# Pooled attention and two MLPs in 3xFP32r on one core: storage of the seven weight forms, weight rings, row copies and batch 1's pooled sums

## The chip, the cores and the metric

The kernel runs on one core of a Trainium2 chip. The metric is the device time of one execution in microseconds (us). Three runs of the kernel before took 1726.25, 1720.11 and 1726.49 us, a median of 1726.25 us.

## The reference

```python
# attention: 8 batches, 8 heads, 576 rows, head 64; keys and values are averaged over 8 rows
k_p = k.reshape(B, H, 72, 8, 64).mean(axis=3)
v_p = v.reshape(B, H, 72, 8, 64).mean(axis=3)
scores = q @ k_p.T / 8;  attn = softmax(scores);  x = attn @ v_p      # x: 4608 tokens x 512
# first MLP (512 -> 2048 -> 512)
h = x @ w_in
y = where(h >= 1, h, where(h <= -1, 0, (h + 1) ** 2 / 4)) @ w_out
# second MLP (512 -> 1536 -> 512)
out = (sigmoid(y @ w_gate) * (y @ w_val)) @ w_out2
```

## The kernel before, in words

Tokens are worked on in nine blocks of 512. An FP32 product is made of three FP32r matmuls: each operand is split into a high and a low part, and `three` (lines 603 to 607) multiplies high by high, high by low, low by high. So nearly every operand costs one copy on ScalarE (the high part) and one subtraction on VectorE (the low part) before TensorE can use it.

**No order is written out.** The program registers operations in a `Plan` with an engine, a cost, a key (the time at which it is due) and the buffers that it reads and writes. `Plan.issue` then simulates the engines with these costs and puts the operations out in the order that it finds: on each engine, among those that could start, the one with the lowest key. The real engines follow that order strictly, each in its own queue. A buffer of a ring (`Buf` with a tag and a number of copies) is taken in the order in which the program created the buffers, unless `fifo=False`: line 98 makes a first user of a ring wait, in the plan, for the first user of the buffer created before it.

The stages, with the stretch of the profiled execution that each takes:

- **To about 165 us, batch 0 and block 0.** `pooled` (line 315) sums keys and values over groups of 8 rows. For batches 0 and 1 (`PE_SUMS = 1`) one transfer loads all 8 rows and TensorE adds them up against an identity matrix (line 349 for keys, line 370 for values). For batches from 2 on, SP loads the first 4 rows (line 328), a transfer on POOL's queue adds the other 4 rows to them (line 329, `accum_op=ALU.add`), and VectorE sums the remaining 4 (line 335). Meanwhile the weights of the first MLP arrive 8 bytes a value and are converted (`weight`, line 550); a copy of each goes back to memory on POOL's queue (line 594), and the buffer f of w_in's conversion, one of 3, comes free when that copy has landed. Block 0's second GEMM runs in plain FP32 (line 735).
- **165 to 710 us, blocks 1 to 6 of the first MLP**, with the attention of the later blocks between their steps. At the end of a block the four PSUM banks `acc` go through two buffers of the ring `raw` to memory (`out_rows`, line 617; `raw` has 2 copies of 4 KB per partition and also takes raw weights and the operands of `prepare1`). The next block's first accumulation waits for the copies at lines 622 and 623.
- **710 to 860 us, block 0 of the second MLP.** `prepare` (line 818) also makes the seven sums of quarters ("forms") of each pair of gate or value column blocks that Strassen's scheme (Winograd's form) needs, splits them, and stores them with one transfer (line 849). Per partition the DRAM tensor holds all seven high parts and then all seven low parts, so a later load of one form (`load_seven`, line 853) takes two runs of 1 KB from each partition.
- **From 860 us, pairs.** Four more rounds use Strassen's scheme on two blocks at a time: 7 products in place of 8. Round 0 ("in") runs blocks 7 and 8 through the first MLP, rounds 1 to 4 ("gv") run pairs of blocks through the second. In a round, `load_one` or `load_seven` fetch one form into the ring `ws` (9 buffers of 256 KB); then `out_pair` (line 964) does the second GEMM with the out weights' forms, loaded by line 982 into the ring `wo` (5 buffers). Each `ws` or `wo` buffer serves 6 matmuls. The splits of the activations are lines 793 and 794, the sums of halves line 970; `A` (line 967) sets how far ahead of the product the split is due: 12 for round 0, 30 for the others.
- **In round 1** (about 1020 to 1145 us) `prepare_out` (line 935) also builds the seven forms of the out weights: 6 times it reloads 512 KB into a `raw` buffer (line 942, due 12 ahead of its sums), sums (line 946), splits into `wo` buffers and stores (line 956, POOL's queue). In every round `input_sums` (line 1124) makes the next round's sums of inputs, twice, each time holding one `raw` buffer and the buffer `bt` (loads at line 1131, stores at line 1138); the next round reads them back at line 1217 and splits them at lines 788 and 789.

Of the kernel before, what the change touches and what calls it, by code (L numbers as in the profile page):

```python
# [18 lines left out]
P = 128  # L19
POOL = 8  # L20
# [22 lines left out]
AHEAD_SPLIT = 12.0  # L43
# [30 lines left out]
class Plan:  # L74
# [7 lines left out]
    def op(self, eng, cost, key, fn, r=(), w=(), after=(), behind=(), nbytes=0, share=1.0, dmas=1):  # L82
        o = Op()
        o.ways = [(eng, cost, fn)] if isinstance(eng, str) else list(zip(eng, cost, fn))
        o.key, o.bytes, o.share, o.dmas = key, nbytes, share, dmas
        o.takes, data, order = [], set(after), set(behind)
        for b in r:
            data |= set(b.writers)
            b.readers.append(o)
        for b in w:  # L90
            if b in r:
                data |= set(x for x in b.readers if x is not o)
            elif b.readers:
                data |= set(b.readers)
                b.readers, b.writers = [], []
            if b.ring and not b.users:
                o.takes.append(b)
                if b.fifo and b.ring in self.last:
                    order.add(self.last[b.ring])
                self.last[b.ring] = o  # L100
            elif b.ring:
                order.add(b.users[0])
            b.writers.append(o)
        for b in set(r) | set(w):
            b.users.append(o)
# [100 lines left out]
def pooled_attention_two_mlps(  # L206
# [75 lines left out]
    AC = {n: ac for n in ("kp", "q", "qT", "mx", "sm", "aq", "aT")}  # L282
# [20 lines left out]
    def due1(s):  # L303
        return T0 + S1 * s
# [10 lines left out]
    def pooled(b, p, T):  # L315
        h0 = 2 * p

        def kv():
            if b == 0:
                return Buf(x_p, "x", 2 * KD, [C, 2, POOL, D], fifo=False)  # L320
            return Buf(kv_p, "kv", 2, [C, 2, POOL if b <= PE_SUMS else POOL // 2, D])

        def load(src, o, key):
            rows = src[b, h0:h0 + 2].rearrange("h (c r) d -> c h r d", r=POOL)
            if b <= PE_SUMS:
                op(SP, 0.475, key, lambda: nc.sync.dma_start(out=o.t, in_=rows), w=[o], nbytes=C * 4096)
# [12 lines left out]
        ks, vs = kv(), kv()  # L339
        kt, vp = kts[b % 2, p], vps[b % 2, p]  # L340
# [3 lines left out]
        if b <= PE_SUMS:  # L344

            def add_keys():
                for r in range(POOL):
                    for h in range(2):
                        nc.tensor.matmul(out=pt.t[D * h:D * h + D, 0:C], lhsT=ks.t[:, h, r], rhs=ident.t[:C, :C],
                                         start=r == 0, stop=r == POOL - 1)  # L350
            op(PE, 1.1, T + 1, add_keys, r=[ks, ident], w=[pt], share=0.3)
# [13 lines left out]
        if b <= PE_SUMS:  # L365
            pv = bank(where)

            def add_values():
                for r in range(POOL):
                    nc.tensor.matmul(out=pv.t[:C, 0:P].rearrange("c (h d) -> c h d", h=2), lhsT=ident.t[:C, :C],  # L370
                                     rhs=vs.t[:, :, r], start=r == 0, stop=r == POOL - 1)
            op(PE, 1.8, T + BEHIND_V, add_values, r=[vs, ident], w=[pv], share=0.6)
# [244 lines left out]
    def out_rows(key, dst, accs, d=()):  # L617
        for i in range(2):
            st = Buf(raw_p, "raw", 2, [P, 2, TB])
# [54 lines left out]
    for j in range(NB1):  # L674
# [66 lines left out]
        out_rows(due1(s + 2) - 4, y_d[j].t, accs, [y_d[j]])  # L741
# [71 lines left out]
    def buf_seven():  # L813
        tag, bufs = (("wa", 2), ("wa", 2), ("wb", 1))[turn[0] % 3]
        turn[0] += 1
        return late(tag, bufs, [P, 2, NMAT, HK], F32R)

    def prepare(n, i, key):
# [4 lines left out]
        def lo(k, k1=None):  # L823
            return sl.t[:, 1, k:k1].bitcast(F32) if k1 else sl.t[:, 1, k].bitcast(F32)
# [21 lines left out]
        split2(key - 3, lambda: sl.t[:, 0, 0:3], lambda: sl.t[:, 1, 0:3], 1.0, sl)  # L846
        split_to(key - 1, lambda: sm.t, lambda: sl.t[:, 0, 3:], lambda: sl.t[:, 1, 3:], 1.3, sm, sl)
        d = seven[2 * i + n]
        op2(PL, 1.0, key + 1, lambda: nc.gpsimd.dma_start(out=d.t, in_=sl.t.rearrange("p s k f -> p (s k f)").bitcast(F32)),
# [3 lines left out]
    def load_seven(n, i, mat, key):  # L853
        w, d = late("ws", 9, [P, 2, HK], F32R), seven[2 * i + n]
        op2(SP, 0.475, key, lambda: nc.sync.dma_start(
            out=w.t.bitcast(F32), in_=d.t.rearrange("p (s k f) -> p s k f", s=2, k=NMAT)[:, :, mat]), r=[d], w=[w], nbytes=P * 2 * HK * 4)
# [37 lines left out]
    for i in range(MP):  # L894
# [4 lines left out]
        for n in range(2):  # L899
            sl, a21 = slots[n]  # L900
            for f in range(2):
                last = []
                for c in range(KD):
                    def mm(c=c, sl=sl, a21=a21, o=banks[n, f], f=f):
                        k = slice(c % 2 * P, c % 2 * P + P)
                        a = [a21.t[:, s, k] if (f, c // 2) == (1, 0) else
                             sl.t[:, s, {(0, 0): 0, (0, 1): 1, (1, 1): 2}[f, c // 2], k] for s in range(2)]
# [27 lines left out]
    def prepare_out(i, key):  # L935
# [5 lines left out]
        for n, d in enumerate((d1, d2)):  # L941
            op2(SP, 0.475, key - 12, lambda n=n, d=d: nc.sync.dma_start(
# [21 lines left out]
    def out_pair(pr, hs, K0, KP):  # L964
        kind, j1, j2 = pairs[pr]
        MP = len(hs)
        A = AHEAD_SPLIT if kind == "in" else 30
# [383 lines left out]
```

## Time and profile before

| what | value |
|---|---|
| runs, us | 1726.25, 1720.11, 1726.49 |
| the profiled execution's own time, us | 1720.69 |
| its span, first to last instruction, us | 1718.8 |
| mean granted TensorE clock | 0.996 |
| matmuls | 8720 |
| DMA traffic | 400.30 MB, mean 233 GB/s, 348713 packets |

The profile is of one execution. A line of it names an engine (PE is TensorE, PEld its weight loads, DVE is VectorE, ACT is ScalarE, POOL is GpSimd, SP the queue that issues most transfers), a line of the kernel, the tile written and the tiles read, and times. A wait is put down to what ended it: `PE acc L605 <- ACT raw L622` is a matmul of line 605 that waited for a copy of line 622. A `q` behind an engine's name means its queue: a waiting or issuing instruction.

### The profile page before, as it was taken

How to read it: one execution, taken by the hardware profiler on the slowest of the kernel's cores; microseconds unless marked ns; L12 is line 12 of the kernel's file. 1: busy time of each engine (PE TensorE's matmuls, PEld its weight loads, DVE VectorE, ACT ScalarE, POOL GpSimd, SP SyncE). 2: the span in 40 equal slices, each digit the busy share in tenths (PEclk: the TensorE clock that was granted, in tenths of full speed). 3: DMA queues.
4: the chain of work that ended last, by engine and by line, in shares of the span. 5: the costliest groups of instructions: out<-in, count | busy, mean ns of one | idle time of the engine just before them, and what ended most of it. 6: DMA issues, size and time to landing. Idle time of an engine off the chain costs nothing.

```text
span 1718.8 us, 26738 instructions
## 1 busy us (share of the span) xinstructions
PE 1686.4 (98%) x8720; PEld 1334.7 (78%) x8720; DVE 1173.1 (68%) x2197; ACT 976.5 (57%) x2173; POOL 223.2 (13%) x346
## 2 busy tenths in 40 slices
PE   7999999999999999999999999999999999999998
PEld 6665777777777777778887787778888888888886
DVE  5896777788887878856767946565447545744476
ACT  5764656676676767654466745464435444544344
POOL 0112221323434122200000002100000000000000
PEclk8999999999999999999999999999999999999999
DMA  8975655777887766648988869997889788867774
GB/s 218 301 216 147 153 133 143 204 213 211 237 240 198 221 194 227 223 153 315 342 278 243 272 206 356 343 367 205 241 248 295 220 239 271 273 202 203 208 219 136
DMA packets 348713, 400.30 MB, mean 233 GB/s; under 512 B 133408, under 2 KB 254240, under 8 KB 347040
## 3 DMA queue, kind: packets, MB, share of 16 engines
q1 hardware_dynamic: 312320, 287.15, 56.3%
q0 software_dynamic: 36256, 111.45, 19.6%
q8 instruction: 70, 1.15, 0.3%
q14 instruction: 67, 0.55, 0.1%
HBM read 276.30 MB, written 112.72 MB: 226 GB/s over the span
## 4 chain that ended last, share of the span: by engine, by line
PE 77%; DMA 11%; DVE 5%; issue 3%; ACT 2%; SPq 2%; POOL 1%; DVEq 0%; POOLq 0%; ACTq 0%
PE h L605 10%; PE h L607 10%; PE h L606 10%; PE acc L605 9%; PE acc L607 9%; PE acc L606 9%; PE a L605 5%; PE a L606 5%; PE a L607 5%; PE acc L735 3%; DMA raw<-in_moe_w_out_dram 2%; DMA q<-in_q_dram 2%; PE a L502 1%; DMA seven<-f 1%; DMA raw<-in_moe_w_gate_dram 1%
## 5 line engine op out<-in xcount | busy, mean ns | idle before, releaser
L794 DVE TENSOR_TENSOR g<-win,g 128x512 fp32r<-128x512 f32 x168 | 114.6, 688 | 120.4 <-ACT g L793 119.4
L605 PE MATMUL h<-x,win 128*128 128x512 f32 x448 | 184.4, 412 | 1.2 <-DVE t L718 1.2
L607 PE MATMUL h<-x,win 128*128 128x512 f32 x448 | 175.0, 391 | 1.2 <-DVE win L537 1.2
L606 PE MATMUL h<-x,win 128*128 128x512 f32 x448 | 175.1, 391 | 0.0
L793 ACT CAST g<-win 128x512 fp32r<-128x512 f32 x168 | 104.3, 623 | 112.9 <-PE acc L607 94.5
L605 PE MATMUL acc<-g,wo 128*128 128x512 f32 x400 | 156.5, 391 | 3.9 <-ACT g L793 2.0
L606 PE MATMUL acc<-g,wo 128*128 128x512 f32 x400 | 155.9, 390 | 0.4 <-DVE g L794 0.2
L607 PE MATMUL acc<-g,wo 128*128 128x512 f32 x400 | 155.7, 389 | 0.0
L605 PE MATMUL acc<-g,wj 128*128 128x512 f32 x384 | 153.9, 401 | 1.6 <-ACT raw L622 1.6
L606 PE MATMUL acc<-g,wj 128*128 128x512 f32 x384 | 150.2, 391 | 0.0
L607 PE MATMUL acc<-g,wj 128*128 128x512 f32 x384 | 149.8, 390 | 0.0
L605 PE MATMUL h<-x,ws 128*128 128x512 f32 x336 | 131.2, 390 | 1.5 <-ACT h L1295 0.8
L606 PE MATMUL h<-x,ws 128*128 128x512 f32 x336 | 131.0, 390 | 0.6 <-DVE x L789 0.6
L607 PE MATMUL h<-x,ws 128*128 128x512 f32 x336 | 130.8, 389 | 0.0
L713 ACT ACTIVATE t<-h,half 128x512 f32<-128x512 f32 x112 | 77.0, 687 | 77.9 <-PE h L607 75.3
L605 PEld LDWEIGHTS h<-x,win 128*128 128x128 f32 x448 | 84.1, 188 | 31.0 <-issue 7.9
L607 PEld LDWEIGHTS h<-x,win 128*128 128x128 f32 x448 | 84.1, 188 | 20.0 <-DVE win L537 1.6
L606 PEld LDWEIGHTS h<-x,win 128*128 128x128 f32 x448 | 84.2, 188 | 18.0 <-issue 2.4
L605 PEld LDWEIGHTS acc<-g,wo 128*128 128x128 f32 x400 | 75.1, 188 | 22.9 <-ACT g L793 2.8
L605 PEld LDWEIGHTS acc<-g,wj 128*128 128x128 f32 x384 | 72.0, 188 | 22.5 <-issue 3.0
L606 PEld LDWEIGHTS acc<-g,wo 128*128 128x128 f32 x400 | 75.1, 188 | 16.4 <-DVE g L794 1.1
L607 PEld LDWEIGHTS acc<-g,wo 128*128 128x128 f32 x400 | 75.1, 188 | 15.7
(296 smaller groups left out, 4040.8 us busy)
## 6 DMA issues: line engine op xcount, KB each, us to landing
ws<-seven SPq DMA_DIRECT2D x392, 256.0 KB
wo<-seven_o SPq DMA_DIRECT2D x144, 256.0 KB
seven<-f POOLq DMA_DIRECT2D x112, 256.0 KB, 4.1
seven<-wa POOLq DMA_DIRECT2D x8, 1792.0 KB, 7.2
wo<-seven SPq DMA_DIRECT2D x56, 256.0 KB
w<-f POOLq DMA_DIRECT2D x52, 256.0 KB, 3.5
raw<-w SPq DMA_DIRECT2D x44, 256.0 KB
seven_o<-wo POOLq DMA_DIRECT2D x42, 256.0 KB, 5.7
```

What stands on the lines that cost most here:

```text
L502: nc.tensor.matmul(out=px.t[D * h:D * h + D, lo:hi], lhsT=vps[b % 2, p].t[:, h], rhs=rhs, start=True, stop=True)
L605: nc.tensor.matmul(out=o, lhsT=wh, rhs=xh, start=start, stop=False, skip_group_check=more)
L606: nc.tensor.matmul(out=o, lhsT=wh, rhs=xl, start=False, stop=False, skip_group_check=more)
L607: nc.tensor.matmul(out=o, lhsT=wl, rhs=xh, start=False, stop=stop, skip_group_check=more)
L713: op(ACT, 0.69, Tg, lambda t=t, hps=hps: nc.scalar.activation(out=t.t, in_=hps.t, func=AF.Relu, bias=half.t, scale=0.5), r=[hps, half], w=[t])
L735: nc.tensor.matmul(out=accs[c].t, lhsT=wj.t[:, c * P:(c + 1) * P], rhs=g.t, start=m == 0, stop=m == M1 - 1)
L793: op2(ACT, cost, key, lambda: nc.scalar.copy(out=out_hi(), in_=val()), r=[src, b], w=[b])
L794: op2(DVE, cost, key + 0.5, lambda: nc.vector.tensor_tensor(out=out_lo(), in0=val(), in1=out_hi().bitcast(F32), op=ALU.subtract), r=[src, ...
```

## The change

The edits, all shown in the diff below:

- **2 KB runs.** The tile and the DRAM tensor of the seven forms are laid out form by form, high part and low part of a form side by side; `load_seven` takes one run of 2 KB from each partition.
- **Two weight rings.** In round 0's out GEMM, every second out weight of its first five products goes into the ring `ws` in place of `wo`.
- **A buffer for half the row copies.** For blocks 0 to 5 `out_rows` takes a buffer `st` of its own for the first two banks; the other half still uses `raw`, but out of the ring's order (`fifo=None`: it neither waits for the buffer created before nor holds the next one back). The copies' due time moves from 4 to 10 ahead, for block 6 too.
- **Batch 1's sums.** Batch 1 is loaded as batches from 2 on: SP brings 4 rows, a transfer on POOL's queue adds the other 4. TensorE then adds up 4 rows in place of 8. The two `kv` buffers shrink from 4 to 2 KB per partition, which is the room that `st` takes.
- **Due times.** The splits of round 1's out GEMM are due 22 ahead in place of 30 (`AHEADS`); the reloads of `prepare_out` 22 ahead in place of 12.

```diff
-AHEAD_SPLIT = 12.0
+AHEADS = {0: 12, 1: 22}
...
                 if b.fifo and b.ring in self.last:
                     order.add(self.last[b.ring])
-                self.last[b.ring] = o
+                if b.fifo is not None:
+                    self.last[b.ring] = o
...
-            return Buf(kv_p, "kv", 2, [C, 2, POOL if b <= PE_SUMS else POOL // 2, D])
+            return Buf(kv_p, "kv", 2, [C, 2, POOL // 2, D])
...
-            if b <= PE_SUMS:
+            if b == 0:
                 op(SP, 0.475, key, lambda: nc.sync.dma_start(out=o.t, in_=rows), w=[o], nbytes=C * 4096)
                 return
...
+        R = POOL if b == 0 else POOL // 2
...
-                for r in range(POOL):
+                for r in range(R):
                     for h in range(2):
                         nc.tensor.matmul(out=pt.t[D * h:D * h + D, 0:C], lhsT=ks.t[:, h, r], rhs=ident.t[:C, :C],
-                                         start=r == 0, stop=r == POOL - 1)
+                                         start=r == 0, stop=r == R - 1)
...
-    def out_rows(key, dst, accs, d=()):
+    def out_rows(key, dst, accs, d=(), early=False):
         for i in range(2):
-            st = Buf(raw_p, "raw", 2, [P, 2, TB])
+            st = buf_a("st", 1, [P, 2, TB]) if early and i == 0 else Buf(raw_p, "raw", 2, [P, 2, TB], fifo=None if early else True)
...
-        out_rows(due1(s + 2) - 4, y_d[j].t, accs, [y_d[j]])
+        n0 = len(plan.ops)
+        out_rows(due1(s + 2) - 10, y_d[j].t, accs, [y_d[j]], j < NB1 - 1)
+        if j < NB1 - 1:
+            att_ops += plan.ops[n0:]
...
-        return late(tag, bufs, [P, 2, NMAT, HK], F32R)
+        return late(tag, bufs, [P, NMAT, 2, HK], F32R)
...
-            out=w.t.bitcast(F32), in_=d.t.rearrange("p (s k f) -> p s k f", s=2, k=NMAT)[:, :, mat]), r=[d], w=[w], nbytes=P * 2 * HK * 4)
+            out=w.t.rearrange("p s f -> p (s f)").bitcast(F32), in_=d.t[:, 2 * HK * mat:2 * HK * (mat + 1)]), r=[d], w=[w], nbytes=P * 2 * HK * 4)
...
-            op2(SP, 0.475, key - 12, lambda n=n, d=d: nc.sync.dma_start(
+            op2(SP, 0.475, key - 22, lambda n=n, d=d: nc.sync.dma_start(
...
-        A = AHEAD_SPLIT if kind == "in" else 30
+        A = AHEADS.get(pr, 30)
...
-                w, g = late("ws", 9, [P, 2, HK], F32R) if last and n and i % 3 else buf_wo(), buf_g() if i % 2 else late("g2", 3, [P, 2, TB], F32R)
+                w, g = late("ws", 9, [P, 2, HK], F32R) if last and n and i % 3 or kind == "in" and n < 5 and i % 2 else buf_wo(), buf_g() if i % 2 else late("g2", 3, [P, 2, TB], F32R)
```

The sums of the values (line 370) change as those of the keys do, and the slices of the seven forms at lines 824, 846, 847, 849 and 907 follow the new layout.

## Rows read from the trace of the kernel before

**Rows 1.** The page, part 1: busy time, share of the span, instructions, of TensorE.
```profile
PE 1686.4 (98%) x8720; PEld 1334.7 (78%) x8720; DVE 1173.1 (68%) x2197; ACT 976.5 (57%) x2173; POOL 223.2 (13%) x346
```

**Rows 2.** Five stretches (us): busy time per engine, PEclk, DMA share, GB/s.
```profile
64.00:165.00 101.00, 100.10 (x563) 62.31 (x564) 84.96 (x177) 62.04 (x156) 22.02 (x31) 1.00 0.71 207
...
900.00:1030.00 130.00, 126.81 (x550) 102.25 (x549) 91.61 (x145) 76.15 (x131) 0.00 (x0) 1.00 0.77 241
1030.00:1145.00 115.00, 108.27 (x464) 87.09 (x463) 74.32 (x146) 62.49 (x127) 22.65 (x42) 0.99 1.01 361
1145.00:1690.00 545.00, 544.49 (x2401) 450.12 (x2400) 305.53 (x473) 253.26 (x438) 0.00 (x0) 1.00 0.80 238
...
1140.00:1143.40 3.40, 3.40 (x10) 2.67 (x9) 3.40 (x7) 3.18 (x6) 0.00 (x0) 0.52 1.07 392
```

**Rows 3.** Waits of TensorE, whole span: total us, times, longest us.
```profile
PE a L606 <- DVE win L789: 2.0, 1, 2.0
PE acc L605 <- ACT raw L622: 1.6, 2, 0.8
...
PE acc L605 <- DMA wo<-seven: 1.5, 5, 0.4
```

**Rows 4.** The chain of waits, 64 to 126 us: start, us, what.
```profile
75.38 1.75 PE a L370 x16
...
83.68 1.15 PE a L349 x32
...
123.23 1.75 PE a L370 x16
```

**Rows 5.** Tile kv, 0 to 170 us: instructions, and who waited for it.
```profile
L326 SPq DMA_DIRECT2D kv<-in_k_dram x4: 317/357/387, 20.0 to 90.5; - x4
...
L329 POOL DMA_DIRECT2D kv<-in_k_dram x4: 1126/1260/1568, 115.9 to 161.8; - x4
...
  POOL kv L329: 13.0, 3
```

**Rows 6.** Line 594, the weight copies: who waited for them.
```profile
  ACT f L574: 4.7, 3
```

**Rows 7.** One stretch (us) of the first pair's out GEMM, columns as rows 2.
```profile
940.00:1005.00 65.00, 61.81 (x263) 48.41 (x262) 55.77 (x89) 43.05 (x75) 0.00 (x0) 1.00 0.78 251
```

**Rows 8.** Tile raw, 1015 to 1140 us: its reloads, and the waits for them.
```profile
L942 SPq DMA_DIRECT2D raw<-w x12: 325/528/857, 1023.6 to 1104.7; - x12
...
  DMA raw<-w: 14.3, 7
```

**Rows 9.** The chain of waits, 1100 to 1145 us: start, us, what.
```profile
1104.71 8.03 DMA raw<-w
...
1142.52 0.43 PE a L607
```

**Rows 10.** Timeline of SP's queue, 1015 to 1145 us: start, us, engine, issue.
```profile
1094.41 1.07 SPq L942 DMA_DIRECT2D raw<-w  x2
...
1103.98 1.17 SPq L942 DMA_DIRECT2D raw<-w  x2
...
1128.62 0.44 SPq L1138 DMA_DIRECT2D sum2T<-raw  x1
1129.17 0.36 SPq L1217 DMA_DIRECT2D x<-sum2T  x1
```

**Rows 11.** DMA queue of SP, 900-940, 1050-1140, 1150-1300 us: packets, MB, share.
```profile
q1 hardware_dynamic: 6359, 10.14, 83.9%
...
q1 hardware_dynamic: 20797, 24.34, 78.6%
...
q1 hardware_dynamic: 32034, 35.14, 78.1%
```

**Rows 12.** Lines 855 and 861, SP's issues: ns min/median/max, first and last start.
```profile
L855 SPq DMA_DIRECT2D ws<-seven x336: 517/518/1577, 928.7 to 1638.2; - x168
...
L861 SPq DMA_DIRECT2D ws<-seven x56: 319/319/1147, 846.8 to 927.4; - x56
```

More of the change, by code (lines that the diff above doesn't have):

```diff
@@ L281, in pooled_attention_two_mlps @@
     e_sb = fixed(ac.tile([P, NT4, 2, 96], F32, name="e_sb"))
-    AC = {n: ac for n in ("kp", "q", "qT", "mx", "sm", "aq", "aT")}
+    AC = {n: ac for n in ("kp", "q", "qT", "mx", "sm", "aq", "aT", "st")}
     NB1 = NB - 2
@@ L346, in add_keys @@
             def add_keys():
-                for r in range(POOL):
+                for r in range(R):
                     for h in range(2):
                         nc.tensor.matmul(out=pt.t[D * h:D * h + D, 0:C], lhsT=ks.t[:, h, r], rhs=ident.t[:C, :C],
-                                         start=r == 0, stop=r == POOL - 1)
-            op(PE, 1.1, T + 1, add_keys, r=[ks, ident], w=[pt], share=0.3)
+                                         start=r == 0, stop=r == R - 1)
+            op(PE, 1.1 * R / POOL, T + 1, add_keys, r=[ks, ident], w=[pt], share=0.3)
         else:
@@ L368, in add_values @@
             def add_values():
-                for r in range(POOL):
+                for r in range(R):
                     nc.tensor.matmul(out=pv.t[:C, 0:P].rearrange("c (h d) -> c h d", h=2), lhsT=ident.t[:C, :C],
-                                     rhs=vs.t[:, :, r], start=r == 0, stop=r == POOL - 1)
-            op(PE, 1.8, T + BEHIND_V, add_values, r=[vs, ident], w=[pv], share=0.6)
+                                     rhs=vs.t[:, :, r], start=r == 0, stop=r == R - 1)
+            op(PE, 1.8 * R / POOL, T + BEHIND_V, add_values, r=[vs, ident], w=[pv], share=0.6)
             op((ACT, DVE), (0.25, 0.25), T + BEHIND_V + 1, (
@@ L823, in lo @@
         def lo(k, k1=None):
-            return sl.t[:, 1, k:k1].bitcast(F32) if k1 else sl.t[:, 1, k].bitcast(F32)
+            return sl.t[:, k:k1, 1].bitcast(F32) if k1 else sl.t[:, k, 1].bitcast(F32)
         op2(SP, 0.475, key - AHEAD_RELOAD, lambda: nc.sync.dma_start(
@@ L845, in prepare @@
         split2(key - 3, lambda: a21.t[:, 0], lambda: a21.t[:, 1], 0.38, a21)
-        split2(key - 3, lambda: sl.t[:, 0, 0:3], lambda: sl.t[:, 1, 0:3], 1.0, sl)
-        split_to(key - 1, lambda: sm.t, lambda: sl.t[:, 0, 3:], lambda: sl.t[:, 1, 3:], 1.3, sm, sl)
+        split2(key - 3, lambda: sl.t[:, 0:3, 0], lambda: sl.t[:, 0:3, 1], 1.0, sl)
+        split_to(key - 1, lambda: sm.t, lambda: sl.t[:, 3:, 0], lambda: sl.t[:, 3:, 1], 1.3, sm, sl)
         d = seven[2 * i + n]
-        op2(PL, 1.0, key + 1, lambda: nc.gpsimd.dma_start(out=d.t, in_=sl.t.rearrange("p s k f -> p (s k f)").bitcast(F32)),
+        op2(PL, 1.0, key + 1, lambda: nc.gpsimd.dma_start(out=d.t, in_=sl.t.rearrange("p k s f -> p (k s f)").bitcast(F32)),
             r=[sl], w=[d], nbytes=P * 2 * NMAT * HK * 4)
@@ L906, in mm @@
                         a = [a21.t[:, s, k] if (f, c // 2) == (1, 0) else
-                             sl.t[:, s, {(0, 0): 0, (0, 1): 1, (1, 1): 2}[f, c // 2], k] for s in range(2)]
+                             sl.t[:, {(0, 0): 0, (0, 1): 1, (1, 1): 2}[f, c // 2], s, k] for s in range(2)]
                         three(o.t, a[0], a[1], xs[c].t[:, 0], xs[c].t[:, 1], c == 0, c == KD - 1)
```

## The prediction

> **What bounds the kernel now.** I read the page's part 1 first, then a table of stretches, then the waits of TensorE, then chain and tiles in the stretches that the edits touch. TensorE is busy for 98% of the span [rows 1], so a gain needs either fewer matmuls or the removal of one of its few waits: span less busy time is 1718.8 - 1686.4 = 32.4 us in all. The table says where these lie [rows 2]: from 1145 to 1690 us TensorE idles 0.5 us of 545, so whatever the change does in rounds 2 to 4 can bring nothing there. From 64 to 165 us it is busy 100.10 of 101: only less matmul work shortens this stretch. From 900 to 1030 it idles 3.2 us, and from 1030 to 1145, in round 1, 6.7 us. In that last stretch the DMA share is 1.01 at 361 GB/s, so transfers are the scarce thing there, and behind it lie 3.4 us at a granted clock of 0.52 (the lower level, 1.2 GHz), right after TensorE's longest wait of the stretch, the 2.0 us for a split of `win` [rows 3]. The other waits that the edits name are 1.6 us for the row copies (line 622, two times) and 1.5 us for `wo` loads (five times) [rows 3].
>
> **Part 1, batch 1's sums.** Four values sums of 1.75 us and four keys sums of 1.15 us, 16 and 32 matmul instructions each, become half as long. On the chain from 64 to 126 us stand three of the values sums and two of the keys sums [rows 4], together 3 x 1.75 + 2 x 1.15 = 7.55 us, so half of it, 3.8 us, goes. The three sums before 64 us I count at nothing: they lie ahead of the stretch in which TensorE is never idle. Added are eight accumulating transfers on POOL's queue, some 1.26 us of POOL each, 10 us in all, where POOL works 22 of 101 us [rows 2, 5]; SP's eight loads stay eight and are half as large. A sum now waits for the load, then for the accumulate. The loads of keys start from 20.0 to 90.5 us and the first and last of the sums on the chain at 75.38 and 123.23 us [rows 4, 5]; what hides the second transfer is that lead, and if it is gone TensorE waits in its own order. What is queued behind the waiting accumulate on POOL are the weight copies of line 594, which free the buffers f; ScalarE waited for them three times, 4.7 us [rows 6]. Bounds: 0 (if another engine takes over; VectorE, the next, is busy 85 of the 101 us [rows 2]) and 4 x 1.45 = 5.8 us. I take 3.8, the chain's own sum.
>
> **Part 2, row copies.** The new buffer lets the first two banks be copied without a free `raw`, and the second half no longer waits for its place in the ring. Gone: the two waits for line 622, 1.6 us [rows 3]. The new order of `raw` can hold up a weight's conversion instead, which runs ahead of its use; that I count at nothing. Bounds 0 and 3.2 us (the same again, for what stood behind TensorE's wait); I take 1.6. The room for the buffer comes from `kv`, and the attention's memory is now kept until block 5's copies are out, before the last attention unit is: nothing.
>
> **Part 3, two weight rings.** From 940 to 1005 us TensorE idles 3.2 of 65 us [rows 7], 1.5 of it for `wo` loads [rows 3]. A product lasts 6 matmuls, so five buffers lead by five products; with every second weight in a ring of nine the lead doubles. I take 1.5 us. The bounds are 0 and 3.2: the rest of the idle time is for splits, and VectorE is busy 55.8 of these 65 us, so it is next in line. Round 1's first `ws` loads, which were issued from 928.7 us on [rows 12], now stand behind these weights in the ring; they are needed only when round 1 begins, after this GEMM, so nothing is due on that.
>
> **Part 4, round 1.** TensorE loses 6.7 us of waiting between 1030 and 1145 us, and 3.4 x 0.48 = 1.6 us at the lower clock [rows 2], 8.3 us together. The tile view says what they come from: VectorE and ScalarE stood idle 14.3 us, seven times, for reloads of the out weights [rows 8], and in the chain such a reload of 8.03 us precedes the last waits [rows 9]. Both engines work in order, so sums and copies that TensorE needs stand behind it. The edit issues the twelve reload transfers up to 10 us earlier. But `raw` has two buffers, and `input_sums` holds one for long: in SP's order the fifth pair of reloads goes out at 1094.41 and the sixth at 1103.98 us, just when the fifth's buffer is given up [rows 10]. For the sixth the ring decides, not the due time, unless the fifth moves first. The smaller lead of round 1's splits (22 for 30) puts the next round's splits ahead of them on VectorE, which aims at the 2.0 us [rows 3]. I take half of 8.3 us, 4.2, because the ring lets the reloads in the middle move and not those at a change of hands. Bounds 0 and 8.3 us; a loss is a rival below.
>
> **Part 5, 2 KB runs.** Each of 336 loads goes from 256 packets to 128. What a packet costs by itself I take from SP's queue in two stretches [rows 11], one with mostly 2 KB loads and one with mostly 1 KB loads: 0.839 x 40 x 16 = 537 engine-us for 6359 packets and 10.14 MB, and 0.781 x 150 x 16 = 1874 for 32034 packets and 35.14 MB. Solved together they give 1.3 ns a packet, the rest goes by bytes. In the full stretch from 1050 to 1140 us, with some 60 such loads, that is 60 x 128 x 1.3 ns / 16 = 0.6 us of DMA time: nothing on TensorE's path. The other end is that cost goes by packets alone: 7680 of that stretch's 20797 packets fewer [rows 11] would take 37% off its queue's work and, at the most, free all of part 4's 8.3 us. I take the low end, which the two rows give. SP's issue falls from 517 to 319 ns [rows 12]; SP waits for buffers in between, so that is hidden by TensorE's own pace.
>
> By the Trainium skill (DMA: Bandwidth & Descriptors, Specifications) runs of 512 B already go at line rate, and a core gets about 358 GB/s of memory bandwidth; so a stretch that is full is full of bytes, which the change does not make fewer. The trace agrees on the packets (1.3 ns) and nearly on the rate (361 GB/s from 1030 to 1145 us [rows 2]). By that rule part 5 is 0, as taken, and part 4 may shrink as well, which is the first rival.
>
> **The sum.** 3.8 + 1.6 + 1.5 + 4.2 + 0 = 11.1 us less than the profiled execution's own 1720.69: 1709.6 us. Its time is 5.6 us under the median shown (1726.25) and at the lowest run (1720.11), so the runs spread by 0.4%; I add 1.4 us of that spread and say **1711 us**.
>
> **Rivals.** First, *round 1 stays full*: reloads issued earlier only take bandwidth from `ws` loads in a stretch with a DMA share of 1.01 [rows 2], and TensorE waits as long for them. Then parts 1 to 3 are left, 6.9 us: 1713.8 us by the profiled time. For it speaks the share; against it, that the waits are put down to engines standing idle for one late transfer [rows 8]. Second, *slower: the sums come too late*. If the earlier reloads take `raw` ahead of `input_sums`, round 2's inputs are late. The place is SP's queue: the last sum is stored at 1128.62 us and the next round's loads of such sums begin at 1129.17, 0.55 us later [rows 10]. A reload holds its buffer some 9.6 us (1103.98 - 1094.41); one put ahead of each of the two sets delays the last by 19 us, of which TensorE waits for nearly all. With the 6.9 us of parts 1 to 3 that gives 1720.7 + 19 - 6.9 = 1733 us. It decides from the point where the last sum lies over 2 us later, against round 1's first product, than now. Against it: `raw` holds no reload for long stretches between the pairs, and the plan knows the ring. Third, *POOL's queue is held*: accumulates waited 13.0 us in three cases for their loads [rows 5], 4.3 each, and the copies behind them free f late. At ScalarE's 1.6 us a case [rows 6] eight cases cost 12.5 us and eat the gain: 1722 us. Against it, POOL idles 79 of the 101 us.
>
> The Trainium skill (SBUF — State Buffer, SBUF: two separate sides) says that a transfer issued from GpSimd can wait for its descriptors while VectorE copies, 3.1 us in place of 0.62. Line 329's 1.1 to 1.6 us beside a busy VectorE [rows 5] does not show that much; eight times the difference would be an estimate of 20 us more of POOL, which its idle time covers, so this would add to the third case only.
>
> **How the numbers follow.** About 0.5%, 8.6 us, is what a measurement of this kernel can tell from no change. Forecast: 0.52. Round 1 stays full: 0.30. Slower by late sums: 0.09. POOL held: 0.09. The forecast's 15 us under the median is over 0.5%; the second and fourth cases, taken against the profiled time, are within it. So faster 0.52, same 0.39, slower 0.09. Low end: all upper bounds, 5.8 + 3.2 + 3.2 + 8.3 = 20.5 us, give 1700; high end: POOL held, or no gain with the runs at the higher level, 1727. The slower case is left out.
>
> **What would show it.** Right: half as many matmuls at lines 349 and 370 of batch 1 and block 0 ending 4 us earlier; no wait for line 622 and none for `wo<-seven`; under half of the idle time for reloads of line 942, no stretch at half clock near 1140 us, SP's `ws` issues at 0.32 us. Wrong: a DMA share still at 1 with TensorE waiting as long from 1030 to 1145 us; `win` or `x` splits waited for longer at round 2's start; ScalarE waiting more for line 594; a wait elsewhere in blocks 1 to 6 that a new order of the plan brought.

## The result and the profile after

The changed kernel takes **1702.96 us** (median of 4 runs, 1700.81 to 1708.59); the kernel before, in the same session, 1723.18 us (1719.9 to 1726.49). The ratio is 0.9888, 95% interval 0.9852 to 0.9923: 19.3 us less. The profiled executions differ by 16.5 us in span (1718.8 and 1702.3). The sum had 11.1 us; the likeliest time, 1711, was 8 us too high, and the range held the measurement.

Where the time went shows in the starts of a few matmuls, the same ones in both traces (us from the start of the span; differences are after minus before):

| mark | before | after | difference | step |
|---|---|---|---|---|
| first matmul of the first weight product | 40.8 | 42.5 | +1.6 | +1.6 |
| end of block 0 | 170.0 | 167.7 | -2.3 | -3.9 |
| first matmul of round 0 | 853.6 | 847.9 | -5.7 | -3.4 |
| first matmul of round 2 | 1134.3 | 1119.5 | -14.8 | -9.1 |
| end of the span | 1718.8 | 1702.3 | -16.5 | -1.7 |

The mark with the largest step, the first matmul of round 2, before and after:

```profile
1134.32 0.39 PE L605 MATMUL h<-x,ws 128*128 128x512 f32 x1
```

```profile
1119.49 0.39 PE L607 MATMUL h<-x,ws 128*128 128x512 f32 x1
```

So part 1's stretch gave 3.9 us (3.8 was forecast), blocks 1 to 6 gave 3.4 (1.6 was forecast), and rounds 0 and 1, where parts 3 and 4 act, gave 9.1, with 1.7 more behind them (5.7 was forecast for both parts). The 1.6 us at the start cannot be put down to the change: in the traces of the changed kernel and its variants below the first mark lies anywhere from 38.2 to 42.5 us. Line numbers after lie a little higher: 605 to 607 became 607 to 609, 622 is 624, 789 is 794, 942 is 947; line 855 is 860.

First the page of the changed kernel: part 1's first line, the granted clock in 40 slices, and the packets.

```profile
PE 1676.4 (98%) x8624; PEld 1329.0 (78%) x8624; DVE 1180.3 (69%) x2201; ACT 972.3 (57%) x2169; POOL 233.5 (14%) x354
...
PEclk8999999999999999999999999999999999999999
...
DMA packets 308904, 400.28 MB, mean 235 GB/s; under 512 B 133920, under 2 KB 174112, under 8 KB 307232
```

Beside [rows 1]: 96 matmul instructions and 10 us of TensorE less, POOL 10 us more, as worked out for part 1; and span less busy time is 25.9 us, where it was 32.4. The slices are too long to show a short dip of the clock (the kernel before has the same row, with its 3.4 us at half clock); the windows below do. The packets were 348713 for the same 400.3 MB.

The stretches of [rows 2], changed kernel, same columns:

```profile
64.00:165.00 101.00, 99.99 (x517) 60.78 (x518) 92.22 (x190) 67.40 (x166) 31.39 (x42) 1.00 0.80 221
...
900.00:1030.00 130.00, 129.80 (x572) 106.77 (x571) 98.06 (x162) 77.73 (x137) 4.98 (x10) 1.00 0.81 261
1030.00:1145.00 115.00, 112.19 (x488) 90.71 (x487) 71.59 (x133) 62.12 (x123) 17.67 (x33) 1.00 1.00 366
1145.00:1690.00 545.00, 544.27 (x2401) 450.11 (x2400) 308.69 (x478) 254.20 (x438) 0.00 (x0) 1.00 0.79 231
...
1140.00:1143.40 3.40, 3.40 (x17) 2.82 (x16) 3.11 (x6) 1.99 (x4) 0.00 (x0) 1.00 0.88 322
```

Look at the counts behind TensorE's busy time, not only at the time. From 1145 to 1690 us both kernels run 2401 matmuls, one per 0.227 us. From 900 to 1030 us the changed kernel runs 572 for 550: 22 more, worth 22 x 0.227 = 5.0 us, though the idle time fell only from 3.2 to 0.2, 3.0 us. From 1030 to 1145 us it runs 488 for 464: 24 more, 5.4 us, at a DMA share as full as before. (The second window is a rough measure, since a kernel that is ahead has more of round 2 in it; experiment 4 counts between the same two matmuls.) The stretch at half clock near 1140 us is gone. Idle time, from which the prediction worked, understates what a stall costs; the row that shows why comes with the one-ring experiment below.

TensorE's waits, changed kernel, whole span, columns as [rows 3]:

```profile
PE acc L403 <- DMA q<-in_q_dram: 7.5, 1, 7.5
...
PE a L607 <- ACT win L793: 1.1, 1, 1.1
PE a L351 <- DMA kv<-in_k_dram: 1.1, 1, 1.1
```

The waits for the row copies and for `wo` are gone; the 2.0 us for `win` (its low part) are now 1.1 for its high part. The largest is the start's, for `q`: 5.8 us before, 7.5 now, about the step of +1.6 in the table; it is 4.0 in the trace of experiment 5, where TensorE has the same order up to the end of block 0, so it varies without the change.

Tile kv, 0 to 170 us, changed kernel, as [rows 5]; then, in a fence of its own, the chain of waits as [rows 4]:

```profile
L330 POOL DMA_DIRECT2D kv<-in_k_dram x7: 1121/1167/1203, 28.7 to 159.6; - x7
...
  POOL kv L330: 29.8, 9
```

```profile
98.78 0.88 PE a L372 x8
...
105.85 0.65 PE a L351 x16
```

The sums are half as long on the chain (0.88 us for 1.75, 0.65 for 1.15). POOL's queue waits twice as long for its loads (29.8 us for 13.0). TensorE waits once for a transfer into `kv`, the 1.1 us in the list above, at 60.2 us; from 64 to 165 us it is as busy as before.

Tile raw, 1000 to 1135 us, and SP's queue, both of the changed kernel, as [rows 8] and [rows 10]:

```profile
L947 SPq DMA_DIRECT2D raw<-w x12: 320/426/859, 1011.4 to 1088.8; - x12
...
  DMA raw<-w: 5.3, 3
```

```profile
1077.92 0.90 SPq L947 DMA_DIRECT2D raw<-w  x2
...
1088.37 0.91 SPq L947 DMA_DIRECT2D raw<-w  x2
...
1112.49 0.32 SPq L1143 DMA_DIRECT2D sum2T<-raw  x1
...
1114.43 0.95 SPq L1222 DMA_DIRECT2D x<-sum2T  x2
```

The last two pairs of reloads go out 10.4 us apart (9.6 before) and 16 us earlier, 5.7 of which the kernel was ahead at the start of round 0 already; idle time for reloads falls from 14.3 to 5.3 us. The last input sum is stored at 1112.49 us and the loads of sums follow 1.9 us later: the sums are not late.

### The profile page after: what moved, and what is told of

Its sections match the earlier page's. It is cut to its first block, busy times and chain, and to the rows that moved or that the text cites. A ratio compares the mean times of both kernels' runs of the same rounds, so it can differ in the third digit from the quotient of the medians.

```text
span 1702.3 us, 26545 instructions
## 1 busy us (share of the span) xinstructions
PE 1676.4 (98%) x8624; PEld 1329.0 (78%) x8624; DVE 1180.3 (69%) x2201; ACT 972.3 (57%) x2169; POOL 233.5 (14%) x354
## 4 chain that ended last, share of the span: by engine, by line
PE 85%; DMA 7%; issue 3%; DVE 3%; ACT 2%; POOL 1%; SPq 0%; POOLq 0%; DVEq 0%; ACTq 0%
PE acc L607 11%; PE h L607 11%; PE acc L609 11%; PE acc L608 11%; PE h L609 11%; PE h L608 11%; PE a L607 4%; PE a L609 4%; PE a L608 4%; PE a L504 2%; PE acc L737 1%; PE a L432 1%; DMA raw<-in_moe_w_gate_dram 1%; DMA raw<-in_moe_w_out_dram 1%; DMA q<-in_q_dram 1%
## 5 line engine op out<-in xcount | busy, mean ns | idle before, releaser
L607 PE MATMUL acc<-g,wo 128*128 128x512 f32 x360 | 140.1, 389 | 0.7 <-ACT g L798 0.7
L609 PE MATMUL acc<-g,wo 128*128 128x512 f32 x360 | 140.1, 389 | 0.0
L608 PE MATMUL acc<-g,wo 128*128 128x512 f32 x360 | 140.0, 389 | 0.0
L607 PEld LDWEIGHTS acc<-g,wj 128*128 128x128 f32 x384 | 72.0, 188 | 21.8 <-issue 5.6
L609 PEld LDWEIGHTS acc<-g,wj 128*128 128x128 f32 x384 | 72.1, 188 | 16.0
L1297 ACT COPY u<-a 128x512 f32<-128x512 f32 x96 | 56.4, 589 | 49.3 <-PE a L609 49.3
L608 PEld LDWEIGHTS acc<-g,wj 128*128 128x128 f32 x384 | 72.2, 188 | 14.1
```

What stands on the lines that cost most here:

```text
L607: nc.tensor.matmul(out=o, lhsT=wh, rhs=xh, start=start, stop=False, skip_group_check=more)
L608: nc.tensor.matmul(out=o, lhsT=wh, rhs=xl, start=False, stop=False, skip_group_check=more)
L609: nc.tensor.matmul(out=o, lhsT=wl, rhs=xh, start=False, stop=stop, skip_group_check=more)
L1297: op2(ACT, 0.6, key, lambda: nc.scalar.copy(out=u.t, in_=b.t), r=[b], w=[u])
```

## The experiments

All ratios are to the kernel before in the same session. Those of the changed kernel, and of the three variants of it that turned out to change nothing, are 0.9888 to 0.9895. The changed kernel's own interval (0.9852 to 0.9923) is wide and touches those of the runs that lost time (2, 4, 5 and 6), so for these the stretches of the traces are given beside the medians.

**1. The 2 KB runs alone, both ways.** Taken out of the changed kernel:

```diff
-        return late(tag, bufs, [P, NMAT, 2, HK], F32R)
+        return late(tag, bufs, [P, 2, NMAT, HK], F32R)
```

with the load and the slices of the old layout. And the same edit the other way round, put into the kernel before.

> The changed kernel with the seven forms stored as before (two runs of 1 KB per partition for a load); the order on every engine is that of the changed kernel. My theory (packets cost 1.3 ns each, runs of 2 KB are worth nothing in time): within 3 us of the changed kernel's 1703 us; line 860's issue back from 0.32 to 0.52 us; idle time of TensorE in round 1 as in the changed kernel, some 3 us. Rival (the 2 KB runs relieve the full stretch): 4 to 8 us slower, 1707 to 1711 us, nearly all of it in round 1, where TensorE would idle 6 us or more.

> The kernel before with the 2 KB runs alone; the order on every engine is that of the kernel before. My theory: the same as before within 3 us (1720 to 1726), TensorE still idle 6 to 7 us in round 1, the reload of line 942 that lands late still in the chain. Rival (2 KB runs matter): 4 to 8 us faster than before, from round 1.

Measured: out of the changed kernel 1704.94 us (4 runs), 0.9895 (0.9874 to 0.9917); into the kernel before 1721.3 us (10 runs), 0.9994 (0.9981 to 1.0007). The issue line of the `ws` loads (ns min/median/max), first with 1 KB runs, then in the changed kernel:

```profile
L860 SPq DMA_DIRECT2D ws<-seven x336: 517/518/1304, 960.1 to 1621.0; - x168
```

```profile
L860 SPq DMA_DIRECT2D ws<-seven x336: 319/319/1573, 960.7 to 1621.3; - x168
```

And the stretches of the kernel before with 2 KB runs: the half clock stays, a little earlier.

```profile
1030.00:1145.00 115.00, 110.51 (x474) 89.30 (x473) 74.70 (x146) 63.07 (x129) 22.69 (x42) 0.99 1.01 369
1138.60:1142.00 3.40, 3.40 (x9) 2.63 (x9) 3.40 (x7) 1.88 (x5) 0.00 (x0) 0.50 1.06 407
```

SP's 0.2 us per issue and half the packets of 336 loads are worth nothing that the runs can tell, in either kernel. The ten more matmuls of this stretch (474 for 464) do not show in the median: they are the spread of single traces.

**2. The reloads at their old due time**, in the changed kernel, and at the new one in the kernel before (there 12 became 22, nothing else).

```diff
-            op2(SP, 0.475, key - 22, lambda n=n, d=d: nc.sync.dma_start(
+            op2(SP, 0.475, key - 12, lambda n=n, d=d: nc.sync.dma_start(
```

> The changed kernel with the reloads of prepare_out due 12 ahead again, as before. My theory (the late reloads make round 1's waits): TensorE idles 5 to 7 us in round 1 in place of 2.8, VectorE and ScalarE wait 10 us or more for raw<-w in place of 5.3, 3 to 5 us slower than the changed kernel. Rival (the ring of two raw buffers sets the reloads, not the due time): reloads go out within 2 us of the changed kernel's and the time stays within 2 us.

> The kernel before with the reloads of prepare_out due 22 ahead alone. My theory: round 1's idle time of TensorE falls from 6.7 to 2 to 4 us and the half-clock stretch goes, 4 to 6 us faster, 1718 to 1720. Rival (it needs the smaller lead of the splits or the second ring too): under 2 us faster.

Measured, old due time in the changed kernel: 1709.06 us (4 runs), 0.9924 (0.9898 to 0.9949), so some 6 us lost by the medians, with intervals that touch. The trace places it: from the first matmul of round 0 to that of round 2 it takes 3.8 us longer than the changed kernel. Its window from 1030 to 1145 us, then its idle time for reloads:

```profile
1030.00:1145.00 115.00, 109.52 (x475) 88.22 (x475) 69.73 (x131) 60.85 (x122) 17.29 (x32) 1.00 1.00 360
```

```profile
  DMA raw<-w: 15.0, 10
```

13 matmuls fewer (475 for 488) are 2.9 us of it, and the idle time for reloads is back. Yet the reloads moved little: the sixth pair goes out at 1090.34 us here and at 1088.37 with the new due time. Two to three microseconds for each of the last four pairs are the whole effect on the loads, since the ring of `raw` decides the rest, as the prediction had it. With the old due time the wait for `win` at round 2's start is back as well:

```profile
PE a L608 <- DVE win L794: 1.9, 1, 1.9
```

In the kernel before, the new due time gives 1722.35 us (10 runs), 0.9981 (0.9963 to 0.9999), about 2 us; I had expected 4 to 6, and the rival (under 2) was nearer. From round 0 to round 2 it takes 279.2 us for 280.7, but two traces of the kernel before that lack this edit (2 KB runs alone, batch 1's sums alone) take 278.5 and 278.7, so in this stretch nothing is shown. What does change is the start of round 2, where the 2.0 us wait for `win` is gone; TensorE's waits there, 1130 to 1160 us:

```profile
PE a L605 <- ACT a L1295: 0.7, 1, 0.7
PE h L606 <- DVE x L789: 0.6, 1, 0.6
```

(This profiled execution had lost 4 us before block 0 ended, so its span is not compared.)

**3. The second due time**, `AHEADS`, back to 30 in the changed kernel.

```diff
-AHEADS = {0: 12, 1: 22}
+AHEADS = {0: 12, 1: 30}
```

> The changed kernel with the splits of round 1's out GEMM due 30 ahead again, as before. My theory: only the last microseconds of round 1 change; TensorE waits some 2 us more for the splits of round 2's inputs and may fall to the lower clock for 3 us, 1 to 4 us slower. Rival: no difference over 1 us, since the late input sums set round 2's start either way.

Measured: 1703.67 us (4 runs), 0.9893 (0.9873 to 0.9913), and from round 0 on every mark of the table above within 0.5 us. TensorE's wait for `win` is 0.5 us, not longer. The edit is worth nothing; my expectation that undoing it would cost 1 to 4 us missed.

**4. The second weight ring**, out of the changed kernel and, alone, into the kernel before.

```diff
-... late("ws", 9, [P, 2, HK], F32R) if last and n and i % 3 or kind == "in" and n < 5 and i % 2 else buf_wo() ...
+... late("ws", 9, [P, 2, HK], F32R) if last and n and i % 3 else buf_wo() ...
```

> The changed kernel with all out weights of round 0 in the ring wo (5 buffers) again. My theory (five buffers lead too little): TensorE waits again for wo loads, 1 to 2 us between 900 and 1030 us, and the time rises by 1 to 3 us to 1704 to 1706. Rival (the splits are what it waited for, and the weights were hidden): no wo wait over 0.5 us and the time within 1 us.

> The kernel before with the second ring for round 0's out weights alone. The run with one ring in the changed kernel lost 7.4 us of span between 848 and 1127 us. My theory: the second ring by itself takes away the waits of round 0's out GEMM (wo loads 1.5, the split 1.3), 2 to 3 us, and what it brings in round 1 (waits for ws loads) needs the earlier reloads as well; 1720 to 1722, 2 to 4 us faster. Rival (the ring is worth its 7 us alone, since it also moves round 1 against its transfers): 6 to 8 us faster, and TensorE idle under 4 us in round 1.

Measured: without the ring 1710.12 us (5 runs), 0.9925 (0.9897 to 0.9953); 7.4 us longer from round 0 to round 2. With the ring alone in the kernel before 1718.01 us (10 runs), 0.9959 (0.994 to 0.9978); 5.9 us shorter there (274.8 for 280.7). Its profiled execution had lost some 6 us in blocks 4 and 5, with 6.8 us at half clock, so its span (1718.2) says little and the stretch is what I compare. Windows of the changed kernel without the ring:

```profile
900.00:1030.00 130.00, 127.58 (x551) 103.62 (x550) 95.84 (x158) 74.16 (x130) 3.23 (x6) 0.99 0.75 247
...
940.00:943.40 3.40, 3.40 (x9) 2.63 (x8) 3.40 (x7) 2.13 (x4) 0.00 (x0) 0.50 0.16 16
1030.00:1145.00 115.00, 109.81 (x477) 88.58 (x476) 70.92 (x135) 62.52 (x125) 19.43 (x36) 1.00 1.00 365
```

and of the kernel before with it:

```profile
900.00:1030.00 130.00, 129.95 (x572) 106.81 (x571) 97.12 (x152) 79.25 (x135) 0.00 (x0) 1.00 0.79 253
1030.00:1145.00 115.00, 109.62 (x473) 87.75 (x473) 73.78 (x146) 61.70 (x127) 22.65 (x42) 1.00 1.02 364
```

In the GEMM's stretch the ring alone moves the count from 550 to 572, all of the 22 matmuls, and taking it out moves it back to 551. For round 1 I count between marks instead. From the first matmul of round 0 to that of round 2 every one of these kernels starts 1188 matmuls, which take 269.7 us at 0.227 us each; what a trace takes beyond that is lost. The table gives the us lost up to the last matmul of round 0's out GEMM, and then from there to the first matmul of round 2:

| | reloads due 12 ahead | reloads due 22 ahead |
|---|---|---|
| one ring | kernel before: 5.7, then 5.4 (all four such traces: 3.9 to 5.8, then 3.0 to 5.4) | kernel before with new due time: 5.3, then 4.2; changed kernel without the ring: 5.3, then 4.0 |
| two rings | kernel before with the ring: 0.7, then 4.4; changed kernel with old due time: 0.9, then 4.8 | changed kernel: 0.9, then 1.1 (all six such traces: 0.7 to 1.2, then 0.7 to 2.0) |

Up to the end of the GEMM the ring alone decides, 4.4 to 5.0 us by these pairs, three times the term. Behind it neither edit alone brings anything that the spread of the traces lets one tell; both together take away 4.3 us. My two expectations (1 to 3 us lost, 2 to 4 won) were too low. Which waits these are, TensorE's waits between 845 and 1145 us without the ring say:

```profile
PE h L607 <- DMA ws<-seven: 1.7, 1, 1.7
PE acc L607 <- ACT g L798: 1.3, 1, 1.3
PE a L607 <- DMA ws<-seven: 1.1, 1, 1.1
PE a L607 <- ACT a L1300: 0.9, 1, 0.9
PE acc L607 <- DMA wo<-seven: 0.9, 3, 0.4
```

The wait that I had priced, `wo`, is a small one among these; in the GEMM itself it stands beside the wait for `g`. Between the same times the kernel before has the same 1.3 us for `g` and 1.6 us for `ws`; the changed kernel has 0.2 us for `ws` and none for `g`. The `g` wait in the timeline of TensorE (start, us, idle time ahead of it in brackets), same run:

```profile
937.04 0.39 PE L608 MATMUL h<-win,ws 128*128 128x512 f32 x1
937.26 0.39 PE L609 MATMUL h<-win,ws 128*128 128x512 f32 x1
938.94 0.50 PE L607 MATMUL acc<-g,wo 128*128 128x512 f32 x1 [1.28 <-ACT g L798]
939.66 0.55 PE L608 MATMUL acc<-g,wo 128*128 128x512 f32 x1 [0.22 <-DVE g L799]
940.01 0.63 PE L609 MATMUL acc<-g,wo 128*128 128x512 f32 x1
940.44 0.63 PE L607 MATMUL acc<-g,wo 128*128 128x512 f32 x1
```

Here is why idle time undercounts. A matmul's row lasts 0.39 us while the next one starts 0.22 us later, so the first 0.17 us of every gap look busy: the start at 938.94 comes 1.68 us after the last, 1.45 late, for 1.28 shown. The next ones start 0.72 and 0.35 us apart, another 0.6 us late with 0.22 shown; and from 940.01 on the starts lie 0.43 us apart, at half clock. In the kernel before, the starts from 930 to 1011 us are 5.7 us late in all, against 0.227 us each, for 3.2 us of idle time and without half clock. Of these the five waits for `wo` make 2.3 us (1.5 shown), and the wait for `g` with the two starts behind it 2.1.

In this run the late cast of `g` (938.28 us) stands on ScalarE behind an activation of the round (937.69 us, line 1270), which itself had to wait for TensorE: with one ring, out products are still interleaved there with the round's last first-layer products. In the changed kernel the activations end at 930.78 and the casts follow each other 1.36 us apart, the pace of six matmuls. That the order, and not the larger number of buffers by itself, removes the waits is read from these traces; no run separates the two. In round 1, the waits tell why it takes both edits. With the ring alone (in the kernel before) no wait for `ws` is listed from 1000 to 1145 us, but TensorE waits 1.4 us for `a` and 1.2 for `win` of the round, which ScalarE and VectorE write. With the early reloads alone (the changed kernel without the ring) `ws` costs 2.8 us. With both, these three waits are 0.8, 0.4 and 0.2 us. Why the ring makes the `ws` loads punctual is open: the first of them goes out at 973.0 us instead of 928.7 when the ring is put into the kernel before, since those buffers now serve the GEMM, and the order differs too.

**5. Row copies as before**, in the changed kernel: both halves in the ring of `raw`, due 4 ahead.

```diff
-        out_rows(due1(s + 2) - 10, y_d[j].t, accs, [y_d[j]], j < NB1 - 1)
-        if j < NB1 - 1:
+        out_rows(due1(s + 2) - 4, y_d[j].t, accs, [y_d[j]], False)
+        if False:
```

> The changed kernel with the row copies through raw again, in ring order and due 4 ahead. My theory: waits of TensorE for line 624 come back, 1 to 3 us between 165 and 700 us, and the time rises by 2 to 4 us (the changed kernel's block 6 began 7.4 us earlier than before's, 1.3 us earlier already at block 2). Rival (those 5 us came from another order of the plan, brought by batch 1's sums): no wait for line 624 and the time within 1 us.

Measured: 1710.88 us (9 runs), 0.9922 (0.9899 to 0.9944): 7.9 us over the changed kernel by the medians (5.9 by the ratios), 4.5 by the profiled span, and round 0 starts 4.8 us later. From the end of block 0 to round 0 it takes 686.7 us; the six traces with the new copies take 678.9 to 682.5, and those with the old ones in the kernel before 683.1 to 686.1 (690.1 in the one with 6.8 us at half clock). The waits of TensorE over the span, then the windows:

```profile
PE a L504 <- ACT e_sb L444: 1.4, 1, 1.4
PE h L607 <- DVE t L720: 1.3, 2, 1.1
...
PE acc L607 <- ACT raw L624: 0.8, 1, 0.8
```

```profile
373.50:376.90 3.40, 3.40 (x8) 2.65 (x9) 3.35 (x8) 2.19 (x6) 1.75 (x2) 0.50 0.79 173
479.30:482.70 3.40, 3.22 (x8) 2.55 (x9) 3.29 (x8) 2.80 (x6) 2.68 (x3) 0.50 0.69 192
165.00:700.00 535.00, 530.53 (x3210) 412.00 (x3209) 426.83 (x914) 363.48 (x997) 160.13 (x233) 0.99 0.70 198
```

The wait for the copies is 0.8 us. The rest is other waits and two stretches at half clock, each 3.4 x 0.5 = 1.7 us; the first begins 1.1 us after the 1.4 us wait for `e_sb` ends (372.4 us), the second 0.2 us before the wait for the copies ends (479.5 us). Idle time from 165 to 700 us is 4.5 us, against 1.8 in the changed kernel.

**6. The new order without the new buffer**: both halves in the two buffers of `raw`, but out of the ring's order.

```diff
-            st = buf_a("st", 1, [P, 2, TB]) if early and i == 0 else Buf(raw_p, "raw", 2, [P, 2, TB], fifo=None if early else True)
+            st = Buf(raw_p, "raw", 2, [P, 2, TB], fifo=None if early else True)
```

> The changed kernel with both halves of the row copies in raw, out of the ring's order, and no buffer of their own. My theory (the ring's order, not its two buffers, made the copies late): no wait for line 624 over 0.5 us, the time within 2 us of the changed kernel's 1703. Rival (the room matters): waits for line 624 of 1 us or more come back with a stretch at half clock, 3 to 7 us slower, as with the old copies (1710.9).

Measured: 1713.58 us (5 runs), 0.9942 (0.9921 to 0.9962), 10.6 us over the changed kernel (9.3 by the ratios); I had expected a loss of at most 2, and the rival (the room matters) held. TensorE's waits:

```profile
PE a L504 <- DVE f L659: 2.7, 1, 2.7
PE acc L607 <- ACT raw L624: 2.1, 3, 1.2
```

Leaving the ring's order without more room is no better than keeping the order (687.6 us from block 0's end to round 0, for 686.7). So the room is needed, and it comes from part 1's smaller `kv`; the new buffer with the ring's order kept was not run. The copies' due time, 4 or 10 ahead, gives the same instructions in the same order, so it has no share.

**7. Batch 1's sums alone**, in the kernel before.

```diff
-            return Buf(kv_p, "kv", 2, [C, 2, POOL if b <= PE_SUMS else POOL // 2, D])
+            return Buf(kv_p, "kv", 2, [C, 2, POOL // 2, D])
...
-            if b <= PE_SUMS:
+            if b == 0:
```

with the loops over 4 rows in place of 8 for batch 1.

> The kernel before with batch 1's sums alone: 4 rows loaded, 4 added by transfers, TensorE adds 4. My theory: block 0 ends 2 to 4 us earlier, as 3.8 us of matmul work leave the chain and VectorE, at 92% in the changed kernel, gives a part back; total 1719 to 1722, 2 to 4 us faster. Rival (POOL's queue is held by the accumulates, the weight copies late): ScalarE waits 8 us or more for the copies, block 0 ends no earlier, time the same or up to 10 us slower.

Measured: 1720.29 us (10 runs), 0.9987 (0.9966 to 1.0007). Block 0 ends at 166.8 us for 170.0, 3.2 us less, and the span is 3.6 us shorter; by the ratio it cannot be told from nothing, and round 0 starts at 852.9 for 853.6. More traces help here, since up to the end of block 0 the kernels with the old sums give TensorE the same order, and so do those with the new ones: from the first mark of the table to that end the five with the old sums take 129.1 to 133.5 us (median 130.7), the nine with the new ones 125.2 to 127.6 (median 126.6). That is 4.1 us. The opposite run, batch 1 whole beside the new buffer, was not tried, since the two use the same room.

**8. The input sums' stores on POOL's queue** instead of SP's, in the changed kernel and in the one before. This was a try at more, on the theory that SP's queue holds the reloads up behind these stores.

```diff
-            op2(SP, 0.475, key + 1, lambda: nc.sync.dma_start(out=d.t, in_=o[0]()), r=[o[1]], w=[d], nbytes=P * TB * 4)
+            op2(PL, 1.0, key + 1, lambda: nc.gpsimd.dma_start(out=d.t, in_=o[0]()), r=[o[1]], w=[d], nbytes=P * TB * 4)
```

> The changed kernel with the stores of the input sums (line 1143) issued by POOL in place of SP, so that no ws load stands behind a store that waits for VectorE. My theory: TensorE waits for ws loads only 0.2 us in the changed kernel, so 0 to 1 us is left to gain: 1702 to 1704. Rival (SP's queue still holds round 1's inputs): round 2 starts 1 us or more earlier and the time falls by 1 to 2 us. On the other side, POOL's stores of the out forms may now wait behind the sums: up to 2 us slower.

> The kernel before with the stores of the input sums issued by POOL. In its trace SP waits 6.8 us in round 1 for VectorE at these stores with ws loads behind them, and TensorE waits 1.6 us for a ws load. My theory: that wait goes (under 0.5 us left), and 1 to 3 us of the total with it. Rival (the load was late for want of bandwidth, with a DMA share of 1.0): a ws wait of 1 us or more stays in round 1 and the time is the same.

Measured: 1704.41 us (4 runs), 0.9889 (0.9864 to 0.9914), and 1724.28 us (10 runs), 1.0003 (0.9988 to 1.0017). Nothing in either. In the kernel before I had expected TensorE's wait for `ws` to go; it is 2.2 us in place of 1.6, and in both kernels the wait for a split of `x` at round 2's start grows (2.9 us for 0.6, and 2.4 for 0.2). Waits of all engines in the kernel before with these stores moved, 1030 to 1145 us:

```profile
POOL sum2T L1138 <- DVE raw L1135: 16.7, 5, 10.3
...
DVE o L946 <- DMA raw<-w: 10.1, 4, 5.9
```

The wait now stands on POOL, and VectorE waits for reloads nearly as long as before (10.1 us for 10.7). SP's queue was not what held them.

No version had a lower median than the changed kernel.

## Why the prediction was right, and where its sum was off

**Part 1** (3.8 us, half of the sums on the chain) was right: 3.9 in the changed kernel's own step, 3.2 alone, 4.1 by the medians of all traces. POOL's accumulates took 1.17 us each, 1.26 was taken.

**Part 2** (1.6 us, at most 3.2) was mis-sized: "Gone: the two waits for line 622, 1.6 us" counts the shown idle time of one wait. The step in the table is 3.4; undoing it costs 4.5 us by the span, 6.5 by the stretch from block 0 to round 0 and 7.9 by the medians. Missing were the other waits that go with the copies' place in the ring, and the half clock that can follow. The new order of `raw`, which I counted at nothing, does not help where no buffer goes with it (run 6); beside the new buffer TensorE has no wait for the copies at all.

**Part 3** (1.5 us) is the term that failed. The step was "I take 1.5 us. The bounds are 0 and 3.2": I priced only the waits put down to `wo`, took idle time for the upper bound, and left the splits out as "next in line". The runs show 5.0 us in the GEMM: the idle time counted too little (2.3 us of late starts for the 1.5 at `wo`), and the splits' wait went with the weights', where with two rings the GEMM's products are no longer interleaved with the round's. That this order is the cause is read from the traces and not tested by itself.

**Part 4** (4.2 us) was right in size and half right in mechanism. In round 1 the earlier reloads bring 3.7 us beside the second ring and nothing that can be told without it, and part 3 had counted nothing of the ring for round 1. So the 4.3 us that round 1 lost less belong to both edits together; that the sum had 4.2 there is in part luck. The lead of 22 for 30 "aims at the 2.0 us" of the `win` split and does nothing. It is the reloads' due time that takes this wait away: it is 1.9 to 2.0 us in all five traces with the old due time and SP's stores, and at most 1.1 in those with the new one.

That the range held is in part luck too: parts 2 and 3 went beyond their own upper bounds, and the low end of the range held because part 4 had been given 8.3 there.

**Part 5** (0) was right in both kernels. The two rows' 1.3 ns a packet held; the end by packets alone did not.

**The rivals.** *Round 1 stays full* was right in its premise and wrong in its result: the DMA share stayed at 1.00 with 366 GB/s, yet TensorE lost 1.1 us in place of 5.4 from the end of round 0's GEMM to round 2. In this kernel a full stretch did not mean that TensorE has to wait as long as before. *Late sums* did not happen (1.9 us from the last store to the loads, with no wait on TensorE's side above 0.2 us for `x`). *POOL held* was right in its first half: nine waits, 29.8 us in place of 13.0, and ScalarE waited 8.7 us in six cases behind the weight copies, for 4.7 in three. Block 0 ended earlier all the same; of all this one wait of 1.1 us for `kv` shows on TensorE.

Without the start, the span is 16.5 + 1.6 = 18.1 us shorter: 3.9 from part 1, 3.4 from part 2, 4.8 from the ring in the GEMM, 4.3 from ring and reloads together in round 1, and 1.7 behind it, where the `win` wait and its half clock went. The costs of undoing single edits must not be added up instead: undoing the ring (7.4) and undoing the reloads (3.8) both give back the shared part of round 1.

The Trainium skill (DMA: Bandwidth & Descriptors, Specifications) had given 0 for part 5 from its line-rate rule, and the runs agree (0.9994, 0.9981 to 1.0007). Its memory limit of about 358 GB/s a core is near what round 1 shows, but round 1 ran a little above it, 366 GB/s over 115 us; the measurement decides.

## What to carry to other kernels

Price a stall by counting matmuls in its stretch against a stretch that runs clean, not by its idle time: in the GEMM here 3.0 us of idle time were 5.0 us of lost matmuls. Count between the same two matmuls of both kernels where one kernel is ahead of the other. Before a wait is priced alone, look at what the same buffer ring does to the order of the work around it; the priced wait was less than half of what the ring gave in the GEMM. A due time moves a transfer only as far as its buffer lets it, so try due time and ring together: in round 1 neither brought anything alone that could be told from the spread, and both together 4.3 us. And look at several traces of one order before a difference of 2 us in one of them is called a gain.

## What the runs showed of the hardware that was not expected

Short stalls were followed by 3.4 us at the lower clock in some runs. Without the second ring, TensorE's start at 938.94 us came 1.45 us late, the next two another 0.6, and from 940.0 to 943.4 us the granted clock was 0.50 (1.2 GHz), with matmul starts 0.43 us apart for 0.22. The same stall in the kernel before, equally long, had no half clock behind it, nor had the changed kernel's 1.1 us wait for `win`. The wait of 1.9 to 2.0 us for `win` at round 2's start had 3.4 us at half clock behind it in the kernel before and in the one with 2 KB runs, and none in three others (the ring alone, batch 1's sums alone, the changed kernel with old due time). So the same wait can cost 1.7 us more or not, and which of the two it was is only seen in the granted clock of its own stretch.

SP's issue of a 256 KB load took 0.52 us with 256 runs and 0.32 us with 128, and neither the DMA share of round 1 (1.03 and 1.00) nor the time followed it.
